# A gated recurrence and its feed-forward layer on one core: all turns of the gates on TensorE instead of DMA transposes, with a new order of the program

## The chip, the cores and the metric

The kernel runs on one core of a Trainium2 chip. The metric is the device time of one execution in microseconds (us), lower is better. Before the change it is 511.61 us, the median of three runs (510.91 to 511.62).

## The reference

Inputs x, r_gate and i_gate have 4 sequences of 5824 steps with 256 channels. A recurrence runs along each sequence, and a feed-forward layer of two products follows, whose output is given in float32.

```python
a_base  = sigmoid(a_param)
log_a   = 8 * sigmoid(r_gate) * log(clip(a_base, 1e-6, 1 - 1e-6))
a_t     = exp(log_a)
norm    = sqrt(maximum(1 - a_t * a_t, 1e-6))
x_gated = norm * sigmoid(i_gate) * x
for t in range(S):
    h = a_t[:, t] * h + x_gated[:, t]     # y[:, t] = h
tokens  = y.reshape(4 * 5824, 256)
out     = ((tokens @ w1) * (tokens @ w2)) @ w3 @ w_out   # 256 -> 1024 -> 1024 -> 256
```

## The kernel before

**Tiling.** The 23296 tokens are cut into chunks: two of 256 (both handled in one pair of tiles, `width(0)` being 512), 44 of 512 and a last one of 256. Inputs come with tokens on the partitions. The scan needs channels on the partitions and time along the row, so two things are turned per chunk: tanh(r) (name `th_r`) and the gated input u = (1 + tanh i) * x. The factors of a half that sigmoid by tanh leaves are put into other constants. w3 @ w_out is folded once at the start into one 1024 x 256 matrix, `wp_sb`.

**One chunk, step by step.** The letters are those of the order list:

- r, i, x: loads by SP's DMA queue (`load`, L151); R: tanh of r on ACT (`tanh_r`, L160 or L162); I: tanh of i on ACT (L168); p: plus one (L173); t: two halves of u (`times`, L189 or L192).
- V, U: the turn of `th_r` and of u. For chunks in `TURN_R` and `TURN_U` it is done on TensorE (`turn_pe`, L200): eight 128 x 128 transposes through a bank of PSUM, tile `ptr`. For all others it is a DMA transpose in SP's queue into an SBUF tile (`turn_dma`, L211; tiles `rt` and `ut`).
- d: a = exp(rate * turned) on ACT (`decay`, L223), once for each half of the channels; s: a * a (`square`, on ACT L231, or DVE or POOL L233); q: the root on ACT (L238); g: max(root, 1e-3) * u on DVE (`gated`, L248 for chunks whose loads have long rows, in two instructions, else L251 in one); h: the scan on DVE (L270); y: the cast to bf16 (`cast`, L280 or L282).
- a, b: the products with w1 and w2 (`up_a`, `up_b`, all recorded at L299) in eight blocks of 128 outputs, two blocks to a pair "mp"; c: copy of the first out of PSUM to bf16, tile `sa` (ACT at L322, DVE at L320); m: its product with the second, tile `g_t`, on DVE (L337).
- D: the product with `wp_sb` (`down`, L357), per 128 tokens eight matmuls of 256 columns; e: copy out of PSUM (`evac`, again L320 or L322), tile `ot`; o: store by SP's queue (L380, the last chunk L376).

**Loads.** `long_rows(c)` is true when both turns of a chunk are on TensorE. Then partition p gets four consecutive tokens, one run of 4 KB; otherwise it gets four tokens that lie 128 apart, four runs of 1 KB. The turned bank then has the time interleaved, and the reader undoes this with a strided access.

**Engines by sets.** Sets of chunk and part choose the engine: `DV_COPY` (c on DVE, else ACT), `DV_EVAC` (e), `DV_SQUARE` and `AC_SQUARE` (s, else POOL), `DV_CAST` and `AC_CAST` (y, else POOL), `DV_PLUS` and `DV_HALF` (p and t on DVE, else POOL), `FOLD_ACT`, `W_ACT` and `W_DVE` (pieces of the weights).

**Order.** The scheduler is manual: the string `ORDER` lists every step, and each engine's and each queue's instructions are issued in that order. Buffers are rings that `RINGS` sizes; a step that takes a slot waits until the slot's last user is done. PSUM has two rings: "pb" with 2 slots for `up_b` and the warm matmuls, and "po" with 4 slots that `up_a`, `down`, the fold of the weights and the turns on TensorE share. `HALVED` says for how many of the four pairs the two first 256-token chunks are handled apart; `warm` (W, L287) are matmuls on the identity that produce nothing used.

Of the kernel before, what the change touches and what calls it, by code (L numbers as in the profile page):

```python
# [23 lines left out]
def kernel(  # L24
# [12 lines left out]
    nc = tc.nc  # L37
# [43 lines left out]
    TURN_R = {0, 2, 3, 4, 7}  # L81
    TURN_U = {0, 2, 3, 4, 5, 6, 7}
    DV_TIMES = {0}
    DV_PLUS = set()
    DV_HALF = set()
    DV_SQUARE = {(0, 0), (0, 1), (5, 1), (9, 0)}
    AC_SQUARE = {(2, 0), (2, 1), (3, 0), (4, 0), (4, 1), (5, 0), (6, 0), (6, 1), (7, 0), (8, 1), (9, 1), (11, 1), (12,
        0), (12, 1), (13, 0), (14, 1), (15, 0), (15, 1)}
    DV_CAST = {(1, 1)}
    AC_CAST = {(1, 0)}  # L90
    DV_COPY = {(0, 0, 0), (0, 1, 0), (1, 0, 0), (1, 1, 0), (2, 0, 0), (2, 0, 1), (2, 1, 0), (2, 1, 1), (2, 2, 0), (2,
        3, 0), (3, 0, 0), (3, 1, 0), (3, 3, 0), (4, 0, 1), (4, 1, 0), (4, 1, 1), (4, 3, 1), (5, 2, 1), (5, 3, 0), (6,
        1, 0), (6, 1, 1), (6, 3, 1), (7, 2, 0), (8, 0, 0), (8, 0, 1), (8, 1, 0), (8, 2, 0), (9, 1, 1), (9, 2, 1), (9,
        3, 0), (9, 3, 1), (10, 0, 0), (10, 3, 0), (11, 0, 1), (11, 1, 0), (12, 2, 0)}
    DV_EVAC = {(0, 0), (0, 1), (4, 1), (5, 1), (6, 1), (9, 0), (9, 1)}
    FOLD_ACT = {('e', 0), ('e', 4), ('e', 5), ('e', 7)}
    FOLD_DMA = set()
    W_ACT = {('w2', 0), ('w3', 3)}
    W_DVE = {('w1', 1)}
# [4 lines left out]
    HALVED = 4  # L104
    RINGS = {"r": 4, "i": 5, "x": 4, "th_r": 3, "u": 2, "rt": 2, "ut": 6, "a": 6, "nrm": 6, "h": 2, "y": 4,
# [3 lines left out]
    def ring(pool, shape, dtype, name, tag):  # L109
        slot = taken[tag] % RINGS[tag]  # L110
        taken[tag] += 1
        return pool.tile(shape, dtype, name=name, tag=f"{tag}_{slot}")
# [6 lines left out]
    def dense(t, n):  # L119
        return t.rearrange("p cb j q -> p (cb j q)")[:, :NCB * n * P].rearrange("p (cb j q) -> p cb j q", cb=NCB, q=P)  # L120
# [8 lines left out]
    def width(c):  # L129
        return CT if c == 0 else sizes[c]  # L130

    def part(c):
        return slice(sizes[0], CT) if c == 1 else slice(0, sizes[c])
# [73 lines left out]
    def turn_dma(c, key, nm):  # L207
        pool, tag = (gates, "rt") if key == "pr" else (held, "ut")
        dst = ring(pool, [P, NCB, 4, P], BF16, name=tag, tag=tag)
        n = sizes[c] // P  # L210
        nc.sync.dma_start_transpose(out=dense(dst, n).rearrange("p cb j q -> p (cb j) q"),  # L211
                                    in_=dense(T[nm, c], n).rearrange("p cb j q -> p (cb j q)"))
        T[key, c] = dense(dst, n).rearrange("p cb j q -> p cb (j q)")
# [204 lines left out]
    def fold_t(mi):  # L418
        if mi in FOLD_DMA:
            T["w3t", mi] = t = ring(ffn, [P, KD, P], BF16, name="w3t", tag="w3t")  # L420
            nc.sync.dma_start_transpose(out=t, in_=T["w3b", mi][:, 0, :])
            return
        pt = ring(psum_o, [P, KD, P], BF16, name="ptw", tag="po")
        for k in range(KD):
            nc.tensor.matmul(out=pt[:, k, :], lhsT=T["w3b", mi][:, 0, k * P:(k + 1) * P], rhs=ident,  # L425
                             is_transpose=True, start=(k == 0), stop=(k == KD - 1))
        T["ptw", mi] = pt
# [46 lines left out]
    def last(c):  # L474
# [5 lines left out]
        "V": lambda c, *half: turn_pe(c, "pr", "thr", *half) if c in TURN_R else turn_dma(c, "pr", "thr"),  # L480
        "U": lambda c: turn_pe(c, "pu", "u") if c in TURN_U else turn_dma(c, "pu", "u"),
# [14 lines left out]
        r0 i0 x0 Lw1.1 Lw1.0 r2 i2 Lw2.0 Lw3.2 x2 E W13 A3. A0. A1. A2. R0.1 R0.0 W3 W10 V0.0 V0.1 I0 t0.1 d0.0 s0.0  # L496
        d0.1 s0.1 q0.0 t0.0 Cw1.1 q0.1 Cw1.0 R2 I2 W5 W8 W0 U0 W4 W11 W6 W12 W7 W9 W2 g0 h0.1 h0.0 y0.1 y0.0 a0.0.1
        a0.1.1 a0.1.0 a0.0.0 V2 W15 Cw2.0 g1 h1.1 h1.0 y1.1 y1.0 d2.1 Lw2.1 Lwo.1 Lwo.0 r3 Cw3.2 d2.0 s2.1 s2.0 q2
        b0.0 c0.0.0 c0.1.0 a1.1.0 m0.0 Ft2 a1.1.1 c1.1.0 b0.1 a1.0.0 a0.2.1 a1.0.1 b1.1 m0.1 Fc2 b1.0 a0.2.0 p2 t2.0
        t2.1 U2 c1.0.0 m1.1 Cw2.1 m1.0 a0.3.1 W14 b0.2 a1.3.1 W1 a1.3.0 c0.2.0 g2 Cwo.1 Cwo.0 r4 Lw3.0 Lw3.5 i3 Lw3.1  # L500
        Lw3.4 x3 Lw3.3 Lw3.6 Lw3.7 r7 m0.2 h2.0 h2.1 R3 a1.2.1 a1.2.0 a0.3.0 c1.3.0 c0.3.0 Fm2 b0.3 b1.2 V3 R4 V4
        c1.2.0 d3.1 d4.0 d3.0 d4.1 m0.3 b1.3 y2 Fe2 m1.2 m1.3 a2.0.0 a2.0.1 b2.0 a2.1.0 c2.0.1 c2.0.0 c2.1.0 m2.0
        Cw3.0 s3.1 Cw3.5 Cw3.1 b2.1 a2.2.1 Ft0 a2.1.1 Fc0 Ft1 c2.1.1 Fc1 s4.0 I3 s4.1 c2.2.1 a2.2.0 Ft5 Fm0 p3 Cw3.4
        c2.2.0 Fc5 m2.1 s3.0 q3 Cw3.3 Fe0 b2.3 Fm1 q4 Fe1 Ft4 t3.0 t3.1 U3 Fc4 g3 h3.0 h3.1 Cw3.6 Cw3.7 b2.2 Fm5 Fm4
        a2.3.1 Ft7 R7 Fe5 Fe4 Fc7 r5 i4 r6 x4 i5 i6 i7 c2.3.1 a2.3.0 Ft3 R5 I4 c2.3.0 Fc3 Ft6 Fm7 y3 a3.2.1 Fc6 Fm3
        m2.3 R6 Fe7 c3.2.1 V7 m2.2 Fe3 d7.1 a3.2.0 c3.2.0 d7.0 b3.2 Fm6 a3.3.1 a3.0.0 a3.3.0 m3.2 Fe6 c3.0.0 I5 c3.3.1
        s7.0 I6 V5 r8 i8 V6 r9 x5 b3.3 d5.1 a3.0.1 d5.0 c3.0.1 c3.3.0 m3.3 p4 t4.0 t4.1 p5 s7.1 U4 a3.1.1 c3.1.1 s5.0
        I7 I8 D0.1 D0.0 b3.0 b3.1 a3.1.0 g4 h4.0 h4.1 s5.1 R8 R9 d6.0 d6.1 p6 y4 p8 t5.0 t5.1 D0.3 D0.2 m3.0 e0.0
        c3.1.0 a4.1.1 b4.1 a4.3.1 D2.0 D2.1 s6.1 q7 e2.0 q5 s6.0 x6 p7 t6.0 t6.1 c4.1.1 e0.1 m3.1 c4.3.1 x7 x8 o0.0
        i10 r11 V9 o2.0 a4.0.1 a4.1.0 c4.0.1 c4.1.0 m4.1 a4.2.0 b4.3 a4.3.0 U5 g5 h5.0 h5.1 c4.2.0 c4.3.0 q6 D2.3 D2.2  # L510
        e2.1 r12 r10 V8 o2.1 o0.1 i9 i11 x10 a4.0.0 U6 D3.0 a4.2.1 D3.1 b4.0 c4.0.0 I10 c4.2.1 e3.0 d9.1 d9.0 m4.3 g6
        y5 t8.1 t7.1 t7.0 m4.0 a5.1.0 b4.2 a5.1.1 a5.0.1 a5.0.0 b5.0 c5.1.1 c5.1.0 c5.0.0 m4.2 h6.1 U7 a5.3.1 c5.0.1
        s9.1 R10 c5.3.1 R11 d8.1 I9 m5.0 g7 h6.0 b5.1 D3.3 b5.3 D3.2 a5.2.1 a5.3.0 e3.1 R12 d8.0 m5.1 c5.2.1 c5.3.0
        h7.1 D4.2 a5.2.0 D4.3 e4.1 m5.3 i13 V10 o3.0 x9 p10 t8.0 y6 p9 s8.0 s9.0 h7.0 b6.0 a6.0.0 a6.0.1 y7 c5.2.0 I11
        I13 a6.2.1 a6.2.0 b5.2 s8.1 c6.0.0 c6.0.1 c6.2.0 D4.1 a6.1.0 D4.0 d10.1 c6.2.1 d10.0 e4.0 q9 a6.1.1 m6.0 m5.2
        U8 o3.1 i12 r15 V11 r13 t9.1 t9.0 U9 V12 a6.3.0 b6.1 c6.1.1 c6.1.0 m6.1 a6.3.1 b6.2 a7.1.1 b6.3 a7.1.0 m6.2
        t10.0 s10.1 p11 t10.1 o4.0 o4.1 r16 i14 i16 c6.3.0 q8 c6.3.1 m6.3 g8 h8.0 h8.1 g9 c7.1.1 c7.1.0 a7.3.0 a7.0.0
        a7.0.1 b7.1 c7.3.0 R15 c7.0.0 c7.0.1 D6.0 D6.1 a7.3.1 D5.0 D6.2 b7.3 D6.3 D5.1 d11.1 c7.3.1 e6.0 s11.1 I12
        d11.0 d12.1 m7.1 h9.1 y8 a7.2.1 a8.2.0 b7.0 e6.1 m7.3 p12 s11.0 p13 s10.0 e5.0 a8.2.1 a7.2.0 c7.2.1 I16 c8.2.1
        s12.1 m7.0 c8.2.0 a8.0.1 b7.2 c8.0.1 c7.2.0 a8.0.0 c8.0.0 m7.2 D5.2 D5.3 b8.0 a8.1.1 d12.0 R13 q10 q11 c8.1.1  # L520
        I14 x11 o6.0 t11.0 t11.1 U10 r14 x12 o6.1 x13 V13 b8.2 D7.1 D7.0 h9.0 m8.0 g10 e5.1 y9 t12.1 V15 U11 o5.0 o5.1
        m8.2 b8.1 a8.1.0 c8.1.0 a9.1.0 a9.0.1 h10.0 h10.1 m8.1 e7.0 R16 c9.1.0 c9.0.1 d13.1 a9.0.0 b9.0 c9.0.0 D7.2
        a8.3.1 a9.1.1 D7.3 c9.1.1 R14 d15.0 e7.1 c8.3.1 y10 p16 a8.3.0 b9.1 d13.0 o7.0 x15 x14 i15 V14 o7.1 r17 t13.0
        p14 s13.1 t12.0 t13.1 m9.0 m9.1 a10.0.0 b8.3 d15.1 c8.3.0 c10.0.0 s12.0 s15.1 a9.2.1 a10.3.1 a10.0.1 b10.0
        a9.2.0 c9.2.1 m8.3 g11 c10.3.1 c10.0.1 m10.0 c9.2.0 d14.0 b9.2 D8.1 a10.3.0 a9.3.1 D8.0 h11.0 c10.3.0 e8.0
        d14.1 I15 D8.2 D8.3 e8.1 V16 d16.0 s13.0 a9.3.0 b10.3 d16.1 c9.3.1 h11.1 m9.2 U12 U13 r19 o8.0 r20 i17 x16 i19
        a10.2.0 a10.2.1 b9.3 a10.1.1 c10.2.1 c10.2.0 R17 m10.3 c9.3.0 m9.3 b10.2 c10.1.1 s14.0 y11 p15 t14.0 s16.1
        t15.1 t15.0 s16.0 t14.1 a10.1.0 a11.0.1 c10.1.0 m10.2 c11.0.1 a11.1.0 a11.3.0 b10.1 a11.0.0 a11.1.1 c11.1.0
        m10.1 q12 s14.1 c11.3.0 c11.0.0 q13 a11.2.0 b11.0 c11.1.1 g12 m11.0 b11.1 D10.3 a11.3.1 D10.2 s15.0 q14
        c11.2.0 c11.3.1 e10.1 a11.2.1 b11.3 D10.0 q15 D10.1 e10.0 c11.2.1 q16 D9.1 h12.0 h12.1 g13 y12 m11.1 h13.1  # L530
        h13.0 a12.0.1 b11.2 D9.2 a12.0.0 D9.0 D9.3 c12.0.1 R19 c12.0.0 U15 x17 U14 o8.1 o10.1 V17 d17.0 I17 r18 r23
# [133 lines left out]
```

## Time and profile before

| | |
|---|---|
| median of the runs | 511.61 us |
| the profiled execution | 510.87 us |
| its span, first to last instruction | 509.1 us |
| PE busy, granted clock | 501.7 us, 1.0 |
| ACT, DVE, POOL busy | 461.5, 431.8, 318.0 us |
| bytes moved | 124.06 MB, 244 GB/s over the span |
| packets under 512 B, under 2 KB, all | 87378, 174036, 178048 |

The profile is one execution on the chip. PE is TensorE's matmuls and PEld its weight loads, which overlap; DVE is VectorE, ACT ScalarE, POOL GpSimd, SP the engine whose queue issues the DMAs. "Idle before" is the time an engine stood empty ahead of a group, and what ended it. The ends of matmuls are modelled, so the distance between the starts of successive groups is a better measure of their cost than the durations.

### The profile page before, as it was taken

What the parts mean: (1) busy time and instruction counts of PE and PEld (TensorE: products, weight loads), DVE (VectorE), ACT (ScalarE), POOL (GpSimd) and SP (SyncE); (2) the same over time, 40 slices, a digit from 0 to 9 for tenths busy, and PEclk for the clock granted to TensorE, in tenths of its full rate; (3) what the DMA queues carried; (4) which work ended last, traced back from release to release, by engine and by line L of the source; (5) the groups of instructions that cost most, each with busy time, mean ns of one, the idle gap of its engine ahead of it and who ended that gap; (6) DMA issues with size and microseconds to landing.
All of it is one profiled execution on the core that took longest, in us unless ns stands there. A gap on an engine that the chain in (4) does not pass through costs nothing.

```text
span 509.1 us, 8891 instructions
## 1 busy us (share of the span) xinstructions
PE 501.7 (99%) x3225; PEld 308.3 (61%) x3225; DVE 431.8 (85%) x417; ACT 461.5 (91%) x708; POOL 318.0 (62%) x269
## 2 busy tenths in 40 slices
PE   7999999999999999999999999999999999999997
PEld 3767665665665656556656556565566655656566
DVE  6999999999999789879979799878877797959762
ACT  7999999998999999999999999998998979888543
POOL 1686677658658937964886973956647568580200
PEclk9999999999999999999999999999999999999999
DMA  8999999999989998896999997899886895252213
GB/s 317 410 411 345 335 316 282 305 286 259 310 220 298 279 285 247 211 302 196 247 305 327 254 286 148 252 243 227 210 246 164 235 298 161 85 166 62 65 51 104
DMA packets 178048, 124.06 MB, mean 244 GB/s; under 512 B 87378, under 2 KB 174036, under 8 KB 178004
## 3 DMA queue, kind: packets, MB, share of 16 engines
q1 hardware_dynamic: 178000, 123.50, 85.4%
q8 instruction: 25, 0.41, 0.4%
q14 instruction: 19, 0.16, 0.1%
q10 hardware_dynamic: 4, 0.00, 0.0%
HBM read 78.91 MB, written 23.86 MB: 202 GB/s over the span
## 4 chain that ended last, share of the span: by engine, by line
PE 92%; ACT 3%; DMA 2%; POOL 1%; DVE 1%; issue 1%; SPq 1%; ACTq 0%; DVEq 0%
PE po L357 30%; PE pb L299 29%; PE pa L299 29%; DMA wf<-in_moe_w_dram 2%; PE pw L436 1%; ACT sa L322 1%; PE ptr L200 1%; PE ptw L425 1%; POOL u_t L192 0%; DVE h_t L270 0%; SPq L151 0%; ACT ot L322 0%; SPq L407 0%; ACT L168 0%; ACT L238 0%
## 5 line engine op out<-in xcount | busy, mean ns | idle before, releaser
L337 DVE TENSOR_TENSOR g_t<-sa,pb 128x1024 bf16<-128x1024 bf16 (+1 forms) x188 | 218.7, 1180 | 58.9 <-PE pb L299 27.6
L299 PEld LDWEIGHTS <-w_sb 128*128 128x128 bf16 x1504 | 146.4, 98 | 144.1 <-issue 1.4
L322 ACT CAST sa<-pa 128x512 bf16<-128x512 f32 (+1 forms) x332 | 179.8, 591 | 27.1 <-PE pa L299 18.9
L299 PE MATMUL pa<-y_t,w_sb 128*128 128x512 bf16 (+1 forms) x752 | 190.2, 372 | 0.2 <-ACT sa L322 0.2
L299 PE MATMUL pb<-y_t,w_sb 128*128 128x512 bf16 (+1 forms) x752 | 184.9, 372 | 0.2 <-ACT w_sb L414 0.2
L357 PE MATMUL po<-wp_sb,g_t 128*128 128x256 bf16 (+1 forms) x1464 | 177.6, 272 | 0.0
L357 PEld LDWEIGHTS <-g_t 128*128 128x128 bf16 x1464 | 142.5, 98 | 39.5 <-issue 0.3
L282 POOL CAST y_t<-h_t 128x1024 bf16<-128x1024 f32 (+2 forms) x47 | 53.8, 1145 | 140.2 <-DVE h_t L270 136.1
L192 POOL TENSOR_TENSOR u_t<-i_t,x_t 128x512 bf16<-128x512 f32 (+1 forms) x90 | 123.3, 1387 | 3.8 <-DMA ut<-u_t 1.8
L270 DVE TENSOR_TENSOR_SCAN h_t<-a_t,h_t,nrm 128x512 f32<-128x512 f32 (+1 forms) x92 | 121.1, 1343 | 1.6
L233 POOL TENSOR_TENSOR nrm<-a_t 128x512 f32<-128x512 f32 x70 | 78.4, 1137 | 7.0 <-ACT a_t L223 4.0
L223 ACT ACTIVATE a_t<-rt,la 128x512 f32<-128x512 bf16 (+1 forms) x82 | 66.1, 823 | 0.0
L322 ACT COPY ot<-po 128x512 f32<-128x512 f32 x84 | 49.1, 589 | 13.2 <-PE po L357 12.9
L173 POOL TENSOR_SCALAR i_t<-i_t 128x1024 f32<-128x1024 f32 (+1 forms) x45 | 55.4, 1233 | 8.3 <-ACT i_t L168 8.3
L251 DVE SCALAR_TENSOR_TENSOR nrm<-nrm,ut 128x1024 f32<-128x1024 f32 (+1 forms) x39 | 53.2, 1365 | 5.2 <-ACT nrm L238 5.2
L168 ACT ACTIVATE i_t<-i_t 128x1024 f32<-128x1024 f32 (+1 forms) x46 | 48.5, 1063 | 0.3 <-DMA i_t<-in_i_gate_dram 0.2
L238 ACT ACTIVATE nrm<-nrm 128x1024 f32<-128x1024 f32 (+1 forms) x47 | 48.4, 1040 | 0.2
L162 ACT ACTIVATE th_r<-r_t 128x1024 bf16<-128x1024 f32 (+1 forms) x41 | 43.5, 1064 | 0.0
L320 DVE CAST sa<-pa 128x512 bf16<-128x512 f32 x36 | 23.5, 684 | 1.4 <-PE pa L299 0.8
L238 ACT ACT_TABLE_LOAD x17 | 21.8, 1283 | 0.4
L287 PE MATMUL warm<-ident 128*128 128x512 bf16 x32 | 10.7, 473 | 1.6 <-DVE ident L441 1.6
L231 ACT ACTIVATE nrm<-a_t 128x512 f32<-128x512 f32 x18 | 11.4, 645 | 0.0
(55 smaller groups left out, 122.1 us busy)
## 6 DMA issues: line engine op xcount, KB each, us to landing
r_t<-in_r_gate_dram SPq DMA_DIRECT2D x45, 512.0 KB, 5.2
i_t<-in_i_gate_dram SPq DMA_DIRECT2D x45, 512.0 KB, 6.0
x_t<-in_x_dram SPq DMA_DIRECT2D x45, 512.0 KB, 5.5
out_dram<-ot SPq DMA_DIRECT2D x90, 256.0 KB, 3.9
wf<-in_moe_w_dram SPq DMA_DIRECT2D x12, 512.0 KB, 10.5
wf<-in_moe_w_out_dram SPq DMA_DIRECT2D x2, 512.0 KB, 10.2
rt<-th_r SPq DMA_TRANSPOSE x41, 4.7
ut<-u_t SPq DMA_TRANSPOSE x39, 4.4
```

What stands on the lines that cost most here:

```text
L173: (nc.vector if c in DV_PLUS else nc.gpsimd).tensor_scalar(t, t, 1.0, 1.0, op0=ALU.add, op1=ALU.mult)
L192: (nc.vector if (c, half) in DV_HALF else nc.gpsimd).tensor_mul(out=u, in0=t, in1=xt)
L223: nc.scalar.activation(out=a, in_=pr, func=AF.Exp, scale=la4[:, cb:cb + 1], bias=la4[:, cb:cb + 1])
L233: (nc.vector if (c, cb) in DV_SQUARE else nc.gpsimd).tensor_mul(out=n, in0=a, in1=a)
L238: nc.scalar.activation(out=n, in_=n, func=AF.Sqrt, scale=-1.0, bias=1.0)
L251: nc.vector.scalar_tensor_tensor(out=n, in0=n, scalar=1e-3, in1=T["pu", c][:, :, cols], op0=ALU.max, op1=ALU.mult)
L270: nc.vector.tensor_tensor_scan(h[:, cb, :], a[:, cb, :], n[:, cb, :], init, ALU.mult, ALU.add)
L282: (nc.vector if key in DV_CAST else nc.gpsimd).tensor_copy(out=y, in_=h)
L299: nc.tensor.matmul(out=dst, lhsT=w_sb[:, cb, m * P:(m + 1) * P], rhs=T["y", gates_of(c)][:, cb, span(c, mp)], start=(cb == 0), stop=(cb == ...
L322: nc.scalar.copy(out=dst, in_=src_ps)
L337: nc.vector.tensor_mul(out=T["g", z][:, 2 * mp:2 * mp + 2, span(c, mp)], in0=T["sa", c, mp][:, :, :w], in1=T["pb", c, mp][:, :, :w])
L357: nc.tensor.matmul(out=po, lhsT=T["g", c][:, k, j * P:(j + 1) * P], rhs=wp_sb[:, k, cols], start=(k == 0), stop=(k == KD - 1), skip_group_ ...
```

## The change

It puts every chunk into `TURN_R` and `TURN_U`, and removes `turn_dma` and the DMA path of the weight fold, which was not in use (`FOLD_DMA` was empty). With that `long_rows` holds for every chunk. The rings `rt` and `ut` go; `th_r` gets 4 slots instead of 3 and `u` 6 instead of 2. The engine sets are new, `HALVED` is 2 instead of 4, and the list `ORDER` is written anew; it has the same steps but for eight calls fewer that come from `HALVED`.

```diff
-    TURN_R = {0, 2, 3, 4, 7}
-    TURN_U = {0, 2, 3, 4, 5, 6, 7}
+    TURN_R = {0, 2, 3, 4, 5, 6, 7, 8, 9, 10, 11, 12, 13, 14, 15, 16, 17, 18, 19, 20, 21, 22, 23, 24, 25, 26, 27, 28,
+        29, 30, 31, 32, 33, 34, 35, 36, 37, 38, 39, 40, 41, 42, 43, 44, 45, 46}
+    TURN_U = {0, 2, 3, 4, 5, 6, 7, 8, 9, 10, 11, 12, 13, 14, 15, 16, 17, 18, 19, 20, 21, 22, 23, 24, 25, 26, 27, 28,
+        29, 30, 31, 32, 33, 34, 35, 36, 37, 38, 39, 40, 41, 42, 43, 44, 45, 46}
...
-    HALVED = 4
-    RINGS = {"r": 4, "i": 5, "x": 4, "th_r": 3, "u": 2, "rt": 2, "ut": 6, "a": 6, "nrm": 6, "h": 2, "y": 4,
+    HALVED = 2
+    RINGS = {"r": 4, "i": 5, "x": 4, "th_r": 4, "u": 6, "a": 6, "nrm": 6, "h": 2, "y": 4,
...
-    def turn_dma(c, key, nm):
-        pool, tag = (gates, "rt") if key == "pr" else (held, "ut")
-        dst = ring(pool, [P, NCB, 4, P], BF16, name=tag, tag=tag)
-        n = sizes[c] // P
-        nc.sync.dma_start_transpose(out=dense(dst, n).rearrange("p cb j q -> p (cb j) q"),
-                                    in_=dense(T[nm, c], n).rearrange("p cb j q -> p (cb j q)"))
-        T[key, c] = dense(dst, n).rearrange("p cb j q -> p cb (j q)")
...
-        "V": lambda c, *half: turn_pe(c, "pr", "thr", *half) if c in TURN_R else turn_dma(c, "pr", "thr"),
-        "U": lambda c: turn_pe(c, "pu", "u") if c in TURN_U else turn_dma(c, "pu", "u"),
+        "V": lambda c, *half: turn_pe(c, "pr", "thr", *half),
+        "U": lambda c: turn_pe(c, "pu", "u"),
...
     ORDER = """
-        r0 i0 x0 Lw1.1 Lw1.0 r2 i2 Lw2.0 Lw3.2 x2 E W13 A3. A0. A1. A2. R0.1 R0.0 W3 W10 V0.0 V0.1 I0 t0.1 d0.0 s0.0
...
+        r0 i0 E A3. W5 A0. W14 A1. A2. R0.0 R0.1 x0 I0 W3 W12 V0.1 V0.0 W9 W6 W10 t0.1 d0.1 s0.1 d0.0 s0.0 q0.0 t0.0
+        U0 g0 h0.0 h0.1 W8 W2 W15 W11 W7 W1 q0.1 g1 h1.0 h1.1 y1.0 r3 i2 r2 R2 V2 W0 Lw1.0 Cw1.0 y0.1 y0.0 a0.0.1 W13
+        a0.1.1 y1.1 a0.1.0 a1.1.0 a0.0.0 I2 p2 c0.1.0 c0.0.0 a1.1.1 c1.1.0 Lw3.2 Lw2.0 Lw1.1 x2 Cw2.0 r4 Lw2.1 Lwo.1
```

How many steps of each kind the sets and the list give to each engine, before and after (a chunk's halves are counted apart where the step is in halves):

| step | before | after |
|---|---|---|
| V on TensorE, by DMA | 6, 41 | 47, 0 |
| U on TensorE, by DMA | 7, 39 | 46, 0 |
| c on ACT, DVE | 332, 36 | 227, 141 |
| e on ACT, DVE (without the last chunk's) | 83, 7 | 64, 26 |
| s on ACT, DVE, POOL | 18, 4, 70 | 49, 8, 35 |
| y on ACT, DVE, POOL | 1, 1, 47 | 14, 6, 29 |
| p on DVE, POOL | 0, 45 | 6, 39 |
| t on DVE, POOL | 2, 90 | 5, 87 |

## The prediction

> **What bounds the kernel now.** I read the page's busy shares and clock first, to see whether one engine is full. Times are microseconds of the span, slices are fortieths of it.
>
> ```profile
> PE 501.7 (99%) x3225; PEld 308.3 (61%) x3225; DVE 431.8 (85%) x417; ACT 461.5 (91%) x708; POOL 318.0 (62%) x269
> ...
> PE   7999999999999999999999999999999999999997
> ...
> PEclk9999999999999999999999999999999999999999
> ```
>
> TensorE is busy in every slice but the first and last, at the full granted clock. Its ends are modelled, so I check this against its own stream, with the timeline and the groups by form:
>
> ```profile
> 38.14 0.59 PE L299 MATMUL pa<-y_t,w_sb 128*128 128x512 bf16 x2
> 38.58 0.61 PE L425 MATMUL ptw<-ident,w_t 128*128 128x128 bf16 x8
> 39.02 0.59 PE L299 MATMUL pa<-y_t,w_sb 128*128 128x512 bf16 x2
> 39.45 1.06 PE L425 MATMUL ptw<-ident,w_t 128*128 128x128 bf16 x16
> 40.35 1.04 PE L436 MATMUL pw<-wo_sb,w3t 128*128 128x256 bf16 x8
> ```
>
> Take the distance from start to start, not the duration. Two 512-column matmuls cost 0.43 to 0.44 (in the chain ten cost 2.16, so 0.216 each); eight transposes of 128 columns cost 0.44, sixteen cost 0.90: 55 to 56 ns each, though each needs a weight load of its own (98 ns by its row). These are the transposes of the weight fold, but a turn of r or u (L200) has the same shape, and sixteen of them take from 24.78 to 25.85. In the chain sixteen 256-column matmuls cost 1.75, so 0.109 each. Now the whole stream: the two up products have 2 x 8 x 2 matmuls for each of 45.5 chunks of 512 tokens, 1456 x 0.216 = 314.5; the down product 182 x 8 = 1456 x 0.109 = 159; fold 64 x 0.109 + 64 x 0.055 = 10.5; 96 turn transposes 5.3; 32 warm matmuls 6.9. Sum 496. The last matmul ends near 506, so TensorE stands truly empty for only 10, almost all before 20.6. There are no hidden holes behind the 99%.
>
> Then the chain and the DMA queue's issues:
>
> ```profile
> PE 92%; ACT 3%; DMA 2%; POOL 1%; DVE 1%; issue 1%; SPq 1%; ACTq 0%; DVEq 0%
> ...
> rt<-th_r SPq DMA_TRANSPOSE x41, 4.7
> ut<-u_t SPq DMA_TRANSPOSE x39, 4.4
> ```
>
> 92% of the end is TensorE. The 80 DMA transposes are in no line of the chain: they take 1.3 of SP's queue each and land 4.4 to 4.7 after issue, and TensorE never waited for one. They are free now.
>
> **The change part by part.**
>
> *Turns onto TensorE.* 41 turns of tanh(r) and 39 of u move from SP's DMA queue to TensorE. Two belong to the 256-token last chunk and need 4 transposes, 78 need 8: 632 transposes. At 55.5 ns each that is 35.1 of TensorE's queue. All of it lies on the engine that sets the end, and no hole takes it: **+35**.
>
> Here two rules of the Trainium skill meet the trace. VectorE: DVE Perf Modes, section "The three transpose paths" with "Rules for kernel authors", advises TensorE for a 128x128 transpose if PSUM may hold the result, with 390 ns against 1309 ns by DMA. By that rule, counting 0.39 against 1.31 for each of 632, one expects a gain. The rows say what matters is whose queue pays: the DMA's time was covered, TensorE's is not, so the trace decides for a loss. And TensorE: Matmul & The Clock Gate, section "Back-to-back issue gap", puts a sustained stream of weight load and 128-column matmul at about 81 ns each. That would make 632 x 0.081 = 51, a time of 564. The start-to-start distances of 55 to 56 ns here differ from it; the measurement is used, and the rule is kept as a high case.
>
> *PSUM slots.* A turn takes a slot of the four-deep "po" ring, which up_a, down and fold use too: per chunk 12 instead of 10. A slot comes free only when both exp (decay, ACT) or both products (gated, DVE) have read it. If they are late, TensorE waits at its fourth allocation after, and everything behind it in its in-order queue, then product on DVE, waits too. No row of steady turns exists. Nearest: 12 turns before 75 us, where the waits view has TensorE waiting for a turn's input three times, 0.8, 0.5 and 0.5. Over 12 turns that is 0.15 each, for 80 turns 12; but all three lie in the first 20.1 us, where buffers are empty, and after 20.6 us there was none. Bounds 0 and 12 (below nothing is excluded: a slot that is taken can't speed TensorE); I take 1, near the later turns.
>
> *ACT, DVE and POOL reassigned.* With rows of before (sa casts 0.596 on ACT, 0.684 on DVE; squares 0.645, 0.682, 1.152 on ACT, DVE, POOL):
>
> ```profile
> L322 ACT CAST sa<-pa 128x512 bf16<-128x512 f32 x324 | 177.1, 596 | 21.9 <-PE pa L299 14.9 <-DVE g_t L337 6.0
> L251 DVE SCALAR_TENSOR_TENSOR nrm<-nrm,ut 128x1024 f32<-128x1024 f32 x38 | 52.5, 1382 | 5.2 <-ACT nrm L238 5.2
> L320 DVE CAST sa<-pa 128x512 bf16<-128x512 f32 x36 | 23.5, 684 | 1.4 <-PE pa L299 0.8
> L248 DVE SCALAR_TENSOR_TENSOR nrm<-nrm,ptr 128x512 f32<-128x512 f32 x8 | 5.1, 681 | 0.0
> ```
>
> DVE: +105 casts 71.8; +19 output copies at 0.680, 12.9; +5 y casts at 0.689 (the weight cast of that size), 3.4; 6 "plus" (bounds 0.69, that cast, and 1.38, the two-input product; I take 1.0), 6; 3 u products at 0.69, 2.1; +4 squares, 2.7; fold and weight pieces -2.5; the gate product becomes two of 0.681 instead of one of 1.382, -0.7. 431.8 + 95.7 = 527.5, 97% of 545. ACT: casts -62.6, copies -11.3, +31 squares 20.0, y casts 12.9, fold 2.4, and exp from the turned bank 0.773 instead of 0.828, -4.4: 418.5, 77%. Changes of ACT's table stay 34 by the listed order. POOL: -35 squares, -18 y casts, -6 plus, -3 products, +1 weight cast: about 246, 45%. None is over TensorE's 544, so their cover is TensorE. Only DVE's is thin. Before, DVE ran at 98% with ACT at 99% from 40 to 80 us, and TensorE had no hole:
>
> ```profile
> 40.00:60.00 20.00, 20.00 (x149) 13.29 (x147) 19.58 (x27) 19.72 (x28) 14.77 (x14) 1.00 1.07 341
> 60.00:80.00 20.00, 20.00 (x144) 12.89 (x142) 19.66 (x20) 19.97 (x30) 12.21 (x10) 1.00 1.14 314
> ```
>
> (Columns: stretch, its length, busy of PE, PEld, DVE, ACT, POOL, clock, DMA share, GB/s.) DVE may also get cheaper: scans have a median of 1.279 but a mean of 1.371 and a maximum of 2.379, and if the long ones stem from the DMA transposes, 88 x 0.09 = 8 comes off. It is off the path, so I count 0 for both, and give a nearly full DVE +1 in the sum only as part of the stalls above.
>
> *DMA.* 80 transposes leave SP (104 of issue time, and waits in front of them of over 100 that held up loads queued behind), and loads of nearly all chunks read 4 KB runs instead of 1 KB. Their cover is TensorE; nothing waits for loads after the start: 0. SP's new order lets stores wait for ot and hold loads behind them, as now (its waits for ot are 96 in all and reach no one).
>
> *The start.* Loads land about every 1.6 (the ninth, a piece of w3, at 15.3). In the new order the first w1 piece is seventh instead of fifth, w2's ninth instead of eighth, x2 eleventh instead of tenth. I estimate the first up product at 13.3 to 14 (now 13.11), the first b at 16.4 (15.22), the first u turn of chunk 2 at 20.9 (ended 20.4 now). Warm matmuls stay 32. Bounds -1 and +4; I take **+1.5**. The end is alike: two strips of the last tile, copied and stored: 0. Halving fewer of the first chunk's tiles changes no column: 0.
>
> Sum: 35 + 1 + 1.5 = 37.5, on the profiled execution's own 510.9 (span 509.1 and 1.8 around it; the median of the runs, 511.6, is 0.7 above): **548.5**.
>
> **The rivals.**
>
> *DVE becomes the bound (0.13).* For it: 97% of the longer span, and it feeds product and scan, on which TensorE waits. Against: the stretches above, and possibly shorter scans. Price: 527.5 at the 98.5% it held from 20 to 80 is 535.5, plus its 8.3 idle in the first 20 us and 12 in the last 30: 556, so 553 to 565.
>
> *Slots of "po" (0.05).* The 12 of above in full: 559.
>
> *Weight loads not covered (0.02).* 81 ns: 564. Against: the distances.
>
> *Faster (0.01).* One mechanism: the turns fall into holes of TensorE's queue between 80 and 480 us, which modelled ends hide, and the loads' longer runs shorten the start. It decides from holes of 35 on. The stream sum leaves 10 in all, at the start. If it were so, 511 less about 4 of the start, 507.
>
> *No effect (0.01).* The turn sets would have to be inert; they choose the branch at L480-481 directly, so TensorE must see 632 more matmuls, unless the changed branch were never taken. 511.6.
>
> **How the numbers follow.** TensorE pays, 0.78: 548.5, its own range 545 to 553. The range goes up into DVE's and the slots' cases, 544 to 560; outside remain some 0.05 of the high cases, 0.02 without loss, and some 0.08 of errors in start and stalls. About 0.2% (1 us) is what a measurement can tell from no change; all cases but two are slower by far more: slower 0.98, same 0.01, faster 0.01.
>
> **What would show it.** Right: L200 with about 728 transposes instead of 96 (records can be missing), 55 to 56 ns apart; PE still 98 to 99% of a span near 546; PE over 90% of the chain; no DMA_TRANSPOSE; DVE near 520, ACT near 420, POOL near 246. DVE's case: idle of TensorE for sa, g_t or y_t in the middle and DVE at 97% or more. Slots: TensorE waiting at L299 or L357 for a_t or nrm. The start: the time of the first pb. Wrong altogether: TensorE's busy share falling well below 97%, or turns standing closer than 55 ns.

## The result, and the profile after

The kernel after takes 550.1 us, median of three runs (548.86 to 550.27), against 511.61: ratio 1.075, 95% interval 1.0722 to 1.0778. It is slower by 38.5. The profiled execution took 548.86, with a span of 547.1, 38.0 more than before.

The page of the kernel after: busy shares, the slices of TensorE and VectorE, and the chain that ended last, by engine and by line.

```profile
PE 533.4 (98%) x3774; PEld 341.7 (62%) x3841; DVE 507.9 (93%) x594; ACT 433.9 (79%) x631; POOL 241.5 (44%) x208
...
PE   7899999999999999999999999999999999999997
...
DVE  6999999999999999899999999999999998889885
...
PE 87%; DVE 4%; DMA 4%; issue 2%; ACT 1%; SPq 0%; POOL 0%; DVEq 0%; ACTq 0%
PE po L368 27%; PE pb L310 27%; PE pa L310 25%; PE ptr L218 7%; DVE g_t L348 2%; DMA wf<-in_moe_w_out_dram 2%; DMA wf<-in_moe_w_dram 2%; PE pw L443 1%; DVE h_t L281 1%; DVE nrm L259 1%; ACT a_t L234 1%; DVE sa L331 1%; PE ptw L432 0%; SPq L169 0%; ACT sa L333 0%
```

TensorE is still full from the second slice to the last but one (a 9 is 90% or more), of a span 38 longer. The turns (L218, L200 before) are now 7% of the chain. A turn in the middle, from the timeline of TensorE after (start, duration, engine, line, operation):

```profile
321.32 0.61 PE L218 MATMUL ptr<-ident,u_t 128*128 128x128 bf16 x8
321.77 0.59 PE L310 MATMUL pa<-y_t,w_sb 128*128 128x512 bf16 x2
...
329.12 0.61 PE L218 MATMUL ptr<-ident,u_t 128*128 128x128 bf16 x8
329.56 1.91 PE L368 MATMUL po<-wp_sb,g_t 128*128 128x256 bf16 x16
```

Start to start, eight transposes take 0.44 to 0.45. Neither the eight weight loads nor a wait for a bank shows there. The source view of L218 counts 728 of them, 96 before:

```profile
L218 PE MATMUL ptr<-ident,th_r x364: 217/219/314, 5.7 to 488.3; 128*128 128x128 bf16 x182
L218 PE MATMUL ptr<-ident,u_t x364: 217/219/230, 9.3 to 517.2; 128*128 128x128 bf16 x182
```

### The profile page after: what moved, and what is told of

The parts are those of the page before. It is cut to its first block, busy times and chain, and to the rows that moved or that the text cites. A ratio compares the mean times of both kernels' runs of the same rounds, so it can differ in the third digit from the quotient of the medians.

```text
span 547.1 us, 10011 instructions
## 1 busy us (share of the span) xinstructions
PE 533.4 (98%) x3774; PEld 341.7 (62%) x3841; DVE 507.9 (93%) x594; ACT 433.9 (79%) x631; POOL 241.5 (44%) x208
## 2 busy tenths in 40 slices
DMA packets 48134, 103.42 MB, mean 189 GB/s; under 512 B 3923, under 2 KB 28373, under 8 KB 48085
## 3 DMA queue, kind: packets, MB, share of 16 engines
q1 hardware_dynamic: 48080, 102.78, 53.4%
## 4 chain that ended last, share of the span: by engine, by line
PE 87%; DVE 4%; DMA 4%; issue 2%; ACT 1%; SPq 0%; POOL 0%; DVEq 0%; ACTq 0%
PE po L368 27%; PE pb L310 27%; PE pa L310 25%; PE ptr L218 7%; DVE g_t L348 2%; DMA wf<-in_moe_w_out_dram 2%; DMA wf<-in_moe_w_dram 2%; PE pw L443 1%; DVE h_t L281 1%; DVE nrm L259 1%; ACT a_t L234 1%; DVE sa L331 1%; PE ptw L432 0%; SPq L169 0%; ACT sa L333 0%
## 5 line engine op out<-in xcount | busy, mean ns | idle before, releaser
L333 ACT CAST sa<-pa 128x512 bf16<-128x512 f32 (+1 forms) x227 | 127.3, 589 | 58.2 <-PE pa L310 36.0
L210 POOL TENSOR_TENSOR u_t<-i_t,x_t 128x512 bf16<-128x512 f32 x87 | 115.9, 1349 | 71.9 <-DMA x_t<-in_x_dram 41.2
L331 DVE CAST sa<-pa 128x512 bf16<-128x512 f32 (+1 forms) x141 | 92.6, 673 | 10.9 <-PE pa L310 8.2
L234 ACT ACTIVATE a_t<-ptr,la 128x512 f32<-128x512 bf16 (+1 forms) x92 | 68.4, 780 | 11.3 <-PE ptr L218 10.1
L333 ACT COPY ot<-po 128x512 f32<-128x512 f32 (+1 forms) x65 | 37.9, 583 | 33.1 <-PE po L368 31.3
L259 DVE SCALAR_TENSOR_TENSOR nrm<-nrm,ptr 128x512 f32<-128x512 f32 (+1 forms) x94 | 58.3, 661 | 4.3 <-PE ptr L218 3.2
L191 POOL TENSOR_SCALAR i_t<-i_t 128x1024 f32<-128x1024 f32 x39 | 46.4, 1192 | 33.1 <-ACT i_t L186 30.4
L244 POOL TENSOR_TENSOR nrm<-a_t 128x512 f32<-128x512 f32 (+1 forms) x35 | 38.7, 1111 | 30.8 <-ACT a_t L234 30.8
L242 ACT ACTIVATE nrm<-a_t 128x512 f32<-128x512 f32 (+1 forms) x49 | 30.8, 643 | 0.1
L218 PEld LDWEIGHTS <-u_t 128*128 128x128 bf16 x364 | 23.8, 98 | 10.8 <-DVE u_t L207 1.8
L218 PE MATMUL ptr<-ident,u_t 128*128 128x128 bf16 x364 | 27.7, 219 | 2.4 <-DVE u_t L207 1.3
```

The source lines that it names most:

```text
L210: (nc.vector if (c, half) in DV_HALF else nc.gpsimd).tensor_mul(out=u, in0=t, in1=xt)
L218: nc.tensor.matmul(out=pt[:, cb - cbs[0], j * P:(j + 1) * P], lhsT=flat(T[nm, c])[:, j, cb * P:(cb + 1) * P], rhs=ident, is_transpose=True ...
L234: nc.scalar.activation(out=a, in_=pr, func=AF.Exp, scale=la4[:, cb:cb + 1], bias=la4[:, cb:cb + 1])
L259: nc.vector.scalar_tensor_tensor(out=n, in0=n, scalar=1e-3, in1=u, op0=ALU.max, op1=ALU.mult)
L331: nc.vector.tensor_copy(out=dst, in_=src_ps)
L333: nc.scalar.copy(out=dst, in_=src_ps)
```

## The experiments

Each run has its own runs of the kernel before on the same chip (medians 511.23 to 511.31). Differences to the kernel after use its 550.1. That one stood beside other runs of the kernel before (511.61), so differences to it of about 1 say little.

**e4: TensorE's added work by itself.**

```diff
 # up_a, in the kernel before
+        lacking = (c not in TURN_R) + (c not in TURN_U)
+        if c > 1 and q == 0 and mp in (0, 2)[:lacking]:
+            for _ in range(2 * width(c) // P):
+                nc.tensor.matmul(out=pp[:, :P], lhsT=ident, rhs=ident, start=True, stop=True)
         up(c, mp, q, pp[:, :width(c)], w1_sb)
```

> The kernel before, unchanged in order, engines, loads and DMA transposes, with 632 extra matmuls of 128 columns (each with its own weight load, of the identity) written into the bank of an up product just ahead of it: TensorE's added work by itself, with no new slot, no new wait for another engine and no change for the others. Theory 1: 511.6 + 35 = 546.7. Theory 2 (the new engine sets make the loss): under 525. [...]

Measured: 545.13, ratio 1.0657 (1.0641 to 1.0672): +33.9 for 632 matmuls, 53.6 ns each. Busy times of the other engines stay as they were (DVE 432.2, ACT 466.4, POOL 312.0). The chain of e4, by engine and line:

```profile
PE 95%; DMA 2%; POOL 1%; issue 1%; SPq 1%; ACT 0%; ACTq 0%
PE po L361 30%; PE pb L299 28%; PE pa L299 27%; PE pa L313 7%; DMA wf<-in_moe_w_dram 2%; PE pw L440 1%; PE ptr L200 1%; PE ptw L429 1%; POOL u_t L192 0%; SPq L151 0%; ACT sa L326 0%; SPq L411 0%; POOL w_t L420 0%; POOL i_t L173 0%; PE warm L287 0%
```

The old order, the old engines and the DMA transposes kept, TensorE's added columns alone give 33.9 of the 38.5. Theory 1 holds; the new engine sets are not needed for this part of the loss. These are plain matmuls of the turns' shape; e1 adds the transposes themselves.

**e1: every turn twice.**

```diff
 # turn_pe
-        for cb in cbs:
+        for cb in [cb for cb in cbs for _ in range(2)]:
```

> The kernel after, every turn's transposes issued twice into the same bank: 728 more transposes in TensorE's queue, nothing else changed. Theory 1 (the loss is TensorE's stream, 55.5 ns a transpose, and nothing hides it): +40, about 590. Theory 2 (VectorE, 93% busy after, sets the end and TensorE has slack): well under half of that, below 570. Theory 3 (the turns' hold of PSUM slots is the price): the hold grows as well, and waits of TensorE for slots add to the 40: over 596.

Measured: 586.65, ratio 1.1467 (1.145 to 1.1484), 36.6 more than after, 50 ns for each of 728. In its timeline sixteen transposes still stand 0.89 apart from what follows, 56 ns each:

```profile
302.08 1.06 PE L218 MATMUL ptr<-ident,u_t 128*128 128x128 bf16 x16
302.97 1.03 PE L310 MATMUL pa<-y_t,w_sb 128*128 128x512 bf16 x3
```

By that spacing the stream should have grown by 40. The waits of the kernel after took up 1.5 of it: TensorE's idle time is 12.2 in e1 (span 584.7 less busy 572.5) and 13.7 after, and nearly all of the difference lies in the first 40 us (4.8 against 6.2). TensorE's busy time grew by 39.1, which is 53.7 ns for each transpose, near the 53.6 of e4. Why the cost comes out 2 ns below the spacing was not found. Theory 1 holds within this; theory 3, with more waits for slots, does not.

**e11 and e10: less and more for VectorE.**

```diff
 # e11: gated
-            for cb in range(NCB):
+            for cb in range(NCB if c < 8 else 1):
 # e10: copy
+    TWICE = set(sorted(t for t in DV_COPY if t[0] >= 8)[::3])
-        copy_to((c, mp, q) in DV_COPY, T["sa", c, mp][:, q, :w], T["pa", c, mp, q][:, :w])
+        for _ in range(2 if (c, mp, q) in TWICE else 1):
+            copy_to((c, mp, q) in DV_COPY, T["sa", c, mp][:, q, :w], T["pa", c, mp, q][:, :w])
```

> The kernel after without the second half of the gate product (max of the root, times u) of chunks 8 to 46: VectorE has 39 instructions and about 25 us less, no other engine gets them; the turn's bank is free after the first half. The part of the computation left out is that product for 128 of the 256 channels. Theory 1 (TensorE's stream sets the end; what VectorE adds in e10 is only the loss of its reserve): within 1 of 550, at best the few us of TensorE's waits in the middle, so 546 to 550. Theory 2 (VectorE sets a part of the end in the kernel after): 538 to 545.

> The kernel after with every third of VectorE's 112 casts of chunks 8 on issued twice: 38 more instructions, 24 to 26 us more on VectorE (97 to 98% busy), nothing else changed. If VectorE at 93% is real cover: within 3 of 550. If it is thin, as the prediction had it, 5 to 15 slower; if VectorE is a full second bound, 24 slower.

e11 measured 548.72, ratio 1.0739 (1.0724 to 1.0755), not to be told from after; VectorE's busy time fell by 18.3 to 489.6. e10 measured 568.96, ratio 1.1126 (1.111 to 1.1141): 18.9 slower for 23.7 more of VectorE. The pages of e11 and of e10, busy shares:

```profile
PE 536.9 (98%) x3841; PEld 342.3 (63%) x3841; DVE 489.6 (90%) x555; ACT 433.5 (79%) x631; POOL 242.2 (44%) x208
```

```profile
PE 539.0 (95%) x3774; PEld 340.4 (60%) x3841; DVE 531.6 (94%) x632; ACT 435.2 (77%) x631; POOL 241.4 (43%) x208
```

Taking work from VectorE gives nothing that can be told, so it does not set the end after. Giving it more costs most of what is given: of 23.7 only about 5 were covered. In e10 TensorE waits for it, by the groups of the two up products (after the second bar: idle time before the group, and what ended it):

```profile
L311 PE MATMUL pa<-y_t,w_sb 128*128 128x512 bf16 (+1 forms) x700 | 187.0, 374 | 7.4 <-DVE sa L332 3.9 <-DVE nrm L260 1.1 <-DVE ot L332 0.6
L311 PE MATMUL pb<-y_t,w_sb 128*128 128x512 bf16 (+1 forms) x721 | 181.5, 374 | 6.2 <-DVE g_t L350 4.4
```

With the waits of the turns and of the down product, 13.7 of TensorE's idle time after the first 40 us ended with VectorE, where the kernel after has 0.9. VectorE's 39 idle microseconds in a span of 547 were reserve for about 5 of this work. A doubled cast also holds its "po" slot longer just where TensorE needs it, and between 200 and 240 us TensorE lost 2.4 with VectorE at 91%. So how much of the 18.9 is VectorE's total and how much the place of the casts was not separated. My expectation of e10 had 5 to 15 for a thin reserve and 24 for none; 18.9 lies between.

**e6: VectorE's casts given to ScalarE.**

```diff
+    DV_COPY -= set(sorted(t for t in DV_COPY if t[0] >= 8)[::2])
```

> The kernel after with 56 of the 112 casts of chunks 8 on that VectorE does given to ScalarE: VectorE has 38 us less work, ScalarE 33 more. Theory 1 (TensorE's stream sets the end): within 2 of 550. Theory 2 (VectorE is a second bound, and the few waits of TensorE in the middle are its doing): 3 to 8 faster.

Measured: 574.71, ratio 1.1233 (1.1214 to 1.1253), 24.6 slower than after. Both theories missed. ScalarE is busy 80% of the span, VectorE 83%, so no share shows it. The timeline of ScalarE in one place does:

```profile
376.62 1.07 ACT L179 ACTIVATE th_r<-r_t 128x1024 bf16<-128x1024 f32 x1
377.70 1.28 ACT L250 ACT_TABLE_LOAD   x1
378.99 2.00 ACT L250 ACTIVATE nrm<-nrm 128x1024 f32<-128x1024 f32 x2
380.90 0.56 ACT L334 COPY ot<-po 128x512 f32<-128x512 f32 x1
381.36 1.07 ACT L334 CAST sa<-pa 128x512 bf16<-128x512 f32 x2
```

and TensorE beside it:

```profile
379.80 0.61 PE L219 MATMUL ptr<-ident,u_t 128*128 128x128 bf16 x8
382.00 1.46 PE L311 MATMUL pa<-y_t,w_sb 128*128 128x512 bf16 x6 [1.59 <-ACT sa L334]
```

For 4.3 us ScalarE does a tanh, a table and two roots; the casts that free "po" slots stand behind them in its queue, and TensorE waits 1.59 for one. That is the price of slots that the prediction named, met here because a cast was moved behind the wrong neighbours. Over the whole run TensorE's waits for casts on ScalarE come to 16.0 (9.4 at `pa`, 3.3 each at `ptr` and `po`), against none after. The rest of the 24.6 was not traced.

**e5: the loads in 1 KB runs again.**

```diff
-        return c in TURN_R and c in TURN_U
+        return c < 8 and c in TURN_R and c in TURN_U
```

> The kernel after with the loads of chunks 8 to 46 in runs of 1 KB again (tokens 128 apart on a partition), the turns still on TensorE; exp then reads its bank and the gate product its inputs without the strided access, and the gate product is one instruction instead of two. Theory 1: loads have cover, no change beyond 1: 549 to 551. Rival (the long runs are worth something on the path): 3 or more slower.

Measured: 549.87, ratio 1.0748 (1.0729 to 1.0766). Packets go from 48134 to 92292, the queue's share of 16 engines from 53.4% to 55.7%, and the time stays. The long runs, less the strided reading that they bring, are worth nothing that can be told here.

**e7 and e9: the first loads.** Pieces of the list of steps. e7 changes the first two lines shown, e9 these and the third:

```diff
-  ... R0.1 x0 I0 ...   y1.0 r3 i2 r2 R2 V2 W0 Lw1.0 Cw1.0 ...
-  ... c1.1.0 Lw3.2 Lw2.0 Lw1.1 x2 Cw2.0 r4 ...
+  ... R0.1 x0 Lw1.0 I0 ...   y1.0 i2 r2 Lw2.0 R2 V2 W0 Cw1.0 ...
+  ... c1.1.0 Lw3.2 Lw1.1 x2 Cw2.0 r3 r4 ...
-  ... d2.0 d2.1 R3 s2.1 Cw1.1 s2.0 q2 ...
+  ... d2.0 d2.1 Cw1.1 s2.1 s2.0 q2 R3 ...
```

> The kernel after with only SP's first loads reordered: the pieces of w1 and w2 that the first products need come fourth and seventh instead of seventh and ninth, x of chunk 2 tenth instead of eleventh, r of chunk 3 after them. The start term of the prediction was 1.5: if the start is paid in full at the end, 1 to 1.5 faster (548.6 to 549.1) with the first b product near 15; if something else in the start is later (the casts of the weights, the first turn of u), no change.

> e7's order of the first loads, and on ScalarE the cast of w1's second piece ahead of tanh of r of chunk 3 (which waited for its later load in e7, with the cast queued behind it: TensorE lost 2.95 there). If the start is paid in full at the end: 1 to 2 faster than after, 548 to 549. If TensorE's later waits take it up: within 0.5 of after's 550.

e7: 551.32, ratio 1.0776 (1.0756 to 1.0795). I had overlooked what stands behind R3: tanh of r of chunk 3 waited for its now later load, and the cast of a w1 piece behind it. The timeline of ScalarE in e7:

```profile
17.92 1.06 ACT L178 ACTIVATE th_r<-r_t 128x1024 bf16<-128x1024 f32 x1 [2.38 <-DMA r_t<-in_r_gate_dram]
18.88 0.61 ACT L242 ACTIVATE nrm<-a_t 128x512 f32<-128x512 f32 x1
19.40 1.03 ACT L425 CAST w_sb<-wf 128x1024 bf16<-128x1024 f32 x1
```

With the cast ahead of it (e9): 549.04, ratio 1.0737 (1.0722 to 1.0751). The median is 1.1 below after's, but the intervals overlap, and the trace shows less. The first b product stands at 16.50 (16.55 after), so the early w2 did not bring it forward. The turn of u of chunk 2 at 19.34 runs without the break of 0.92 that it has after, but TensorE then waits 0.70 for a piece of w2, and in both kernels for a piece of w_out (`wo_sb`, 0.86 and 0.99). The turn of r behind that wait starts at 25.80, and at 26.04 after. So 0.24 of the start was won back; the rest of the 1.1 is not shown to come from it.

**e12: four warm matmuls less, in the kernel before.**

```diff
-    WARM = [2] * 16
+    WARM = [0 if i in (1, 14) else 2 for i in range(16)]
```

> The kernel before without four of its 32 matmuls that only keep TensorE busy, those at 20.6 and 21.7 us in a stretch where TensorE has real work queued: 4 x 0.216 = 0.86 of stream. Theory 1: 510.7, at the edge of what can be told. Rival (TensorE waits for the next inputs there anyway): 511.5.

Measured: 511.38, ratio 1.0001 (0.9993 to 1.0009). Of the 0.86 of stream, 0.53 stands in its trace as waits (0.27 for g_t at 21.67, 0.26 for a weight cast at 23.62). In the first 24 us TensorE follows its inputs, in contrast to the middle of the run.

**e2, e3, e8: fewer turns on TensorE.** In e2 and e3 the kernel after with turns by DMA again (`turn_dma` put back), in e8 the kernel before with four more:

```diff
-    TURN_U = <all>        # e2; e3 both sets
+    TURN_U = {0, 2, 3, 4, 5, 6, 7}
-    TURN_R = <all>        # e3
+    TURN_R = {0, 2, 3, 4, 7}
-    TURN_R = {0, 2, 3, 4, 7}             # e8, from the kernel before
-    TURN_U = {0, 2, 3, 4, 5, 6, 7}
+    TURN_R = {0, 2, 3, 4}
+    TURN_U = {0, 2, 3, 4}
```

> The kernel after with its new order and engine sets, but the turns of u by DMA where they were before (39 of them, 308 transposes off TensorE; those chunks' loads go back to 1 KB runs). Theory 1: -17, about 533, plus waits where the order gives the DMA too little time. Theory 2: VectorE's work is the same, so it stays within 5 of 550. Theory 3: more than the stream comes back, 525 or less, since 39 slots of PSUM are no longer taken.

> The kernel after with its new order and engine sets, but both turns by DMA as before: 632 transposes off TensorE, 1 KB runs again, one buffer instead of two for the folded weights' turned piece. What is left is the new order by itself. Theory 1: 550 - 35 = 515, with some more where the order leaves the DMA transposes too little time. Theory 2: VectorE, with about 510 of work, does not fit into 515 and holds it at 530 or more. Theory 3: about 505 to 510.

> The kernel before with four more turns by DMA (r of chunk 7, u of chunks 5, 6 and 7), 32 transposes off TensorE: the change's own direction reversed by a small step. Theory 1: -1.8, about 509.8. Rival (in this stretch the DMA engines are full and the order leaves no time for 4.5 us of landing): waits take it back or more, 511 to 515.

Measured: e2 600.78 (ratio 1.1745, 1.1705 to 1.1784), e3 644.06 (1.2596, 1.2544 to 1.2648), e8 528.27 (1.0325, 1.0306 to 1.0345). The work went off TensorE and the time rose, by 51 and 94 over after, and in e8 by 17 over before. Other engines now wait for a turn to land: the waits of e3, all engines and then TensorE's queue (total, times, longest; "issue" is a wait that the profile gives to no one).

```profile
PEld L316 <- issue: 122.4, 122, 13.1
ACT a_t L240 <- DMA rt<-th_r: 85.6, 16, 12.2
DVE nrm L268 <- DMA ut<-u_t: 54.2, 12, 11.6
```

```profile
PE pa L316 <- ACT sa L339: 42.2, 13, 9.8
PE pb L316 <- DVE g_t L354: 42.1, 22, 12.8
```

exp waits up to 12.2 for its turn, the casts stand behind exp on ScalarE, and TensorE waits for the casts' slots. In e8 two DMA transposes stand together in SP's queue for 7.25; exp of chunk 7 waits 3.63 for its turn, and the loads behind them wait too. Two pieces of its chain in order of time (start, length, what):

```profile
38.23 8.38 DMA rt<-th_r
...
46.63 0.03 ACT a_t L223
```

TensorE's two longest waits in e8 come later, 3.35 for `y_t` at 72.33 and 6.37 for `g_t` at 82.94; the path from the transposes to them was not followed to its end.

So the new order by itself, free of the price of turns, could not be measured: with its turns by DMA it takes longer than with them on TensorE. Besides the order, e2 and e3 differ from the kernel before in buffers: the turned u has 3 and 2 slots (`ut`), where the kernel before has 6, and e3 has one slot of `w3t` instead of two. What part of their loss is the order and what part the fewer slots was not separated. e8, which keeps the old rings, shows that the old order too has no room for four more DMA transposes where they were put.

## Why the prediction was right, point by point

- **The time**: 548.5 for 550.1, and 548.86 in the profiled execution, whose own 510.87 was the base. The difference of spans, 38.0, stands against a sum of 37.5. By the spans of before, e4 and after, and by TensorE's idle time, it is 34.2 for the added columns, 2.0 for the start, 1.1 for stalls in the middle, and 0.7 not traced. The first term was 0.8 too high and the start 0.5 too low, so that the sum is closer than its parts is luck.
- **The turns, +35**: confirmed. e4 puts them at 33.9 by its medians, and the spacing of 55 to 56 ns holds after. The 81 ns that the Trainium skill states (TensorE: Matmul & The Clock Gate, section "Back-to-back issue gap"), 563 to 564 as a time, does not hold here: e4 has 53.6 ns of time for each. Its advice to transpose on TensorE (VectorE: DVE Perf Modes, section "Rules for kernel authors") did not bring a gain: it prices the operation, not the queue that pays. One sign that the prediction set was missed: TensorE was to have over 90% of the chain after, and has 87% (95% in e4).
- **PSUM slots and stalls, +1 of 0 to 12**: right in size for the order as written, less so in kind. Between 40 and 520 us TensorE is empty for 4.3 after and for 3.2 in e4; in both traces some matmul records are missing (67 and 65), which leaves gaps of about 0.26 in a stretch of 40 us, so the difference of 1.1 is what counts. Of it 0.7 is one wait for `g_t` at 263.34, a slot of "pb", and 0.2 a wait of a turn for a cast. Waits for exp or the gate product, which were to be the price of a turn's slot, are listed only at weight loads, 0.7 in all for the gate product. e6 and e10 show that the small number belongs to this order: one kind of cast moved, and 24.6 come.
- **The start, +1.5**: the marks came as forecast. The first up product stands at 13.59 (forecast 13.3 to 14), the first b product at 16.55 (forecast 16.4, 15.22 before), and the turn of u of chunk 2 was done at 20.94 (forecast 20.9). TensorE's idle time in the first 40 us is 6.2, and 4.1 before and 4.2 in e4: 2.0 were lost. But in the first 20 us it worked as long as before (15.90 and 16.01). The loss stands behind, in the wait for that u and in 0.99 for `wo_sb` at 25.17, which the prediction did not have.
- **Cover by TensorE**: e11 shows that VectorE does not set the end. But the reason I gave, that no engine's total is over TensorE's 544, is not sufficient: e6 has both totals at 80 to 83% and loses 24.6. The rival in which VectorE becomes the bound was not what happened, yet in e10 its cover ended after about 5 us of further casts.
- **VectorE 527, ScalarE 418**: 507.9 and 433.9. Both errors fit one cause: I added and took off whole durations, in a busy time in which consecutive instructions overlap (in e6 above, a copy starts at 380.90 while the two roots before it end at 380.99). e10's 38 more casts, 0.682 each by their row, added 23.7, so 0.62 each. For 124 casts and copies that is 8 of the 20; "plus" took 0.785, not 1.0, 1 more. The remaining 11 on VectorE and the 15 on ScalarE were not traced. The 8 that I had held possible from shorter scans did not come: without any DMA transpose their mean is 1.356, against 1.371.
- **DMA and SP, 0**: right. The waits did not vanish, they moved: SP's stores now wait 299 for `ot` (195.7 for ScalarE's, 103.3 for VectorE's), the loads behind them come late, and POOL waits for x (and longer still for the scan's h):

```profile
POOL y_t L293 <- DVE h_t L281: 103.2, 18, 18.1
POOL u_t L210 <- DMA x_t<-in_x_dram: 41.2, 6, 18.2
```

  POOL is busy 44% and TensorE waited for its u 0.9 once, in the start. That "its waits reach no one" was thus wrong by one step of the chain, and right at its end.

## What to carry to other kernels

When one engine is full, price a change by what it adds to that engine's queue, start to start, and treat work that is hidden elsewhere as free, as long as the order leaves it time: 80 transposes that take some 4.5 us each to land held up nothing on the path by DMA, and 0.44 each on TensorE cost 34 to 35 in all, but four more by DMA in the same order cost 17. Busy shares say which engine is full, not how much the others can take: an engine at 93% in strict order took 5 of 23.7 us of further work, and one at 79% took 56 casts more at a cost of 24.6. An order written for certain latencies goes badly with others, so single switches turned back in it measure the misfit as well; to isolate a cost, add it to the old order, as e4 did.

## What the runs showed of the hardware that was not expected

Where TensorE waited long, its granted clock fell as well. The slices of e3, busy share and granted clock in tenths:

```profile
PE   7779966867695595859798969957889998899998
...
PEclk9899989897899699789999979986999999999999
```

The mean clock of e3 is 0.937 and that of e2 0.966, with TensorE busy 82 and 89% of the span; it is 1.0 after and in e1 and e4, at 98%. So a part of what stalls cost there is slower matmuls after them; how much was not separated. Long or crowded waits seem to count, not their sum. In e8 a wait of 6.37 ended at 82.94, and the 5 us from 80 on have a clock of 0.50. In e6 two waits of 1.53 and 1.33 ended at 204.76 and 207.12, and the clock from 208 to 212 is 0.50; but a wait of 2.81 that ended at 367.63 left it at 1.0. e10, whose waits after the first 40 us are 1.2 at most, keeps 1.0 although it lost 18.9. No run varied this alone, so no rule follows.

The Trainium skill, TensorE: Matmul & The Clock Gate, section "What's actually happening", has the throttled clock as the default, which activity releases. The start of the kernel after goes with that, from TensorE's timeline:

```profile
2.30 3.59 PE L298 MATMUL warm<-ident 128*128 128x512 bf16 x8
5.69 1.02 PE L218 MATMUL ptr<-ident,th_r 128*128 128x128 bf16 x8
```

The first eight 512-column matmuls take 3.39, or 0.42 each, about twice the 0.216 of later ones, although the clock given for these first microseconds is 1.0.
